# Keys and queries of the first parity by seven block products in place of eight

## The chip, the cores and the metric

The kernel runs on one core of a Trainium2 chip. The metric is device time in microseconds (us) for one execution of the whole program. Before the change three runs gave 600.47, 600.63 and 602.79 us, so the median is 600.63 us. The profile comes from one further execution, which took 599.87 us.

## The reference

The layer mixes a sliding, dilated attention (32 heads of 16 channels, a window of 8 keys, two positions apart) with a gated feed-forward layer. `x` is 2048 x 512 in float32.

```python
g = _sigmoid((x * gate_w).sum(-1, keepdims=True))
qkv = x @ wqkv                                  # 512 x 1536: keys, queries, values of 32 heads
logits = einsum("bhsd,bhswd->bhsw", q, k[idx]) * scale    # idx = pos - 2 * arange(8)
a = einsum("bhsw,bhswd->bhsd", softmax(logits), v[idx]) @ wo
b = (gelu(x @ w_gate) * (x @ w_up)) @ w_down              # F = 1792
return g * a + (1 - g) * b
```

## The kernel before

Each float32 operand of a matrix product is split into a high and a low part (`split`: a rounding copy `hi`, mostly on ACT, and a subtraction `lo = raw - hi`, mostly on DVE). A product then takes three matmuls: hi by hi, lo by hi, hi by lo.

Tokens are cut by parity (even and odd positions never attend to each other), and the kernel works through parity 0 and then parity 1, with 1024 tokens in each: two blocks of 512 tokens (`BT` = 4 tiles of 128). The 512 channels are four chunks `kc` of 128. The input `x` of a parity is a 2 x 2 block matrix: a11, a12 are block 0 with chunks 0-1 and 2-3, a21, a22 are block 1.

Several of the matrix products are done in Strassen's way, with seven block products in place of eight: the four sums s1 to s4 of x's blocks and t1 to t4 of the weight's blocks are made on DVE (`sum_x` or `sums_x`, `combine_b`, `make_v`, `combine`), split, and multiplied: a11 b11, a12 b21, s1 t1, s4 b22, s2 t2, s3 t3, a22 t4. This is how the values (`values`), the gate and up products (`gate_up`, L837) and the keys and queries of parity 1 (`keys`, `key_one`, `key_mm`) are computed. One block product of the keys and queries is 4 tiles x 2 chunks x 3 = 24 matmuls of 512 columns. One block product of the values is 24 matmuls of 258 columns.

The keys and queries of parity 0 go the plain way, in two halves of the heads (`hh`, weight blocks `cb` 0 and 2). The first half is the opening of the kernel: 8 tiles x 4 chunks x 3 = 96 matmuls (`qkv_mm`, L357), whose results `take_first` copies out, partly straight into the attention's tile `kq`. The second half is `project_one`, another 96 matmuls on L357, placed as `pieces` inside the first two of the 14 steps of the feed-forward loop (`ffn`, `gate_up`).

In order of the program: opening (L1109 to L1133), sums of x and the first three value operands, `values(0)` with its seven products (L408), the 14 feed-forward steps of parity 0 (products L778, down products L820), then `keys`, `values(1)` and the feed-forward steps of parity 1, the output product (L1050) and the end.

The attention itself runs on DVE (`scores`, `softmax`, `mix`: L569 to L622), in eight units: four of each parity. It is a generator from which the other code pulls: `pull(n)` adds n to a credit and emits attention instructions until their stated costs have used it up. The credits are constants in the code (`PACE` in the feed-forward steps, per parity). The first unit can start once the first half of the keys is there (`done.add((0, 0))`), it can only be mixed with the values once `values(0)` is through, and units 2 and 3 of a parity need the second half of the heads. Emitted attention instructions get a priority that lies 150 instructions behind (`BEHIND`).

A scheduler orders the instructions of each engine on a simulated timeline by priority; on the chip each engine runs its list in that order. SP issues nearly all loads and stores, POOL the ones that add into their destination. PSUM has eight banks: four of tag `p` and `acc0` to `acc3`. Tiles of one tag share a fixed number of buffers (`BUFS`), so a new tile waits until the old one's readers are done.

The steps to be followed: `room_v` says where the split value operands lie (tags `c`, `g1`, `g0`), `room_b` the same for key operands (`g1`, `d`), `load_v` and `load_b` load weights, `store_b` stores keys and queries, on POOL with an addition where a second product is added in DRAM.

Of the kernel before, what the change touches and what calls it, by code (L numbers as in the profile page):

```python
# [16 lines left out]
P = 128  # L17
# [15 lines left out]
PACE = (0.9, 1.22)  # L33
# [11 lines left out]
def tile_gated_mix(ctx: ExitStack, tc: tile.TileContext, xt, wqkv, wff, wo, out):  # L45
# [24 lines left out]
    idle = bank("p")  # L70
    for _ in range(WARM):
        nc.tensor.matmul(idle[:, :P], warm, warm, start=True, stop=True)
# [45 lines left out]
    def split_x(par, blk, kc, cols=((0, 512),), copy=None, pinned=False):  # L118
        if blk and kc < 2:
            X[par, blk, kc] = tl("rt", F32R), tl("rt", F32R)  # L120
# [6 lines left out]
    def sums_x():  # L127

        for n in ("s1", "s2", "s4", "s3"):
            for kc in range(2):  # L130
                XOP[n, kc] = pair("S")
        for kc in range(2):
            a11, a12, a21, a22 = (XR[kc][:, i * 512:(i + 1) * 512] for i in range(4))
            nc.vector.tensor_tensor(a22, a21, a22, op=OP.add)
            nc.vector.tensor_tensor(a21, a11, a21, op=OP.subtract)
            nc.vector.tensor_tensor(a11, a22, a11, op=OP.subtract)
            nc.vector.tensor_tensor(a12, a12, a11, op=OP.subtract)
            for n, x in ("s1", a22), ("s2", a11), ("s4", a12), ("s3", a21):
                split(nc.vector, *XOP[n, kc], x)
                yield  # L140

    def rooms():

        def of(*tags):
            for tag, n in tags:
                t = tl(tag, F32R)
                w = 512 if n == 4 else WA
                yield from (t[:, i * w:(i + 1) * w] for i in range(n))
        cols = of(("g1", 4))
        for _ in range(2):  # L150
            yield next(cols), next(cols)
        for _ in range(2):
            yield pair("S")
        for _ in range(KC):
            yield pair("d")

    def load_kq_weights(raw, kc):
        nc.sync.dma_start(raw[:, :512], wqkv[0, kc // 2, :, kc % 2 * 512:kc % 2 * 512 + 512])

# [3 lines left out]
    def load_cb(cb, kc, tag, room, late=False):  # L163
        hi, lo = WC[cb, kc] = next(room)
        raw = tl(tag)[:, :512]

        queue = nc.scalar if tag == "c" and not kc else nc.sync
        queue.dma_start(raw, wqkv[cb // 2, kc // 2, :, kc % 2 * 512:kc % 2 * 512 + 512])
        return lambda: split(nc.vector, hi, lo, raw, held if late else None)

    VW, VR, VO, SLOT = 2 * WQ, {}, {}, []

    def room_v(par):

        large, small = [("g1", 3), ("g0", 3)], [("c", 1)] * 4
        for tag, n in small + large if par else large[::-1] + small:
            t = tl(tag, F32R)
            SLOT.extend(t[:, i * WA:i * WA + VW] for i in range(n))  # L180
        for i, n in enumerate(("b11", "b21", "t1", "b22", "t2", "t3", "t4")):
            VO[n] = SLOT[i % 5 * 2:i % 5 * 2 + 2]
        SLOT.clear()

    def load_v():

        t = pool.tile([P, 2 * NP - 1, UC], F32, name="v").rearrange("p a c -> p (a c)")
        u = pool.tile([P, 2, BT * UC], F32, name="tb").rearrange("p a c -> p (a c)")
        places = [t[:, i * VW:(i + 1) * VW] for i in range(3)] + [u[:, :VW]]
        for n, raw in zip(("b11", "b21", "b12", "b22"), places):  # L190
            VR[n] = raw
            a, b = int(n[1]) - 1, int(n[2]) - 1
            nc.sync.dma_start(raw, wqkv[b, 2, :, a * VW:(a + 1) * VW])
# [78 lines left out]

    def sum_x(kc, n):
        a11, a12, a21, a22 = (XR[kc][:, i * 512:(i + 1) * 512] for i in range(4))
        o, a, b, op = {"s1": (a22, a21, a22, OP.add), "s3": (a21, a11, a21, OP.subtract),
                       "s2": (a11, a22, a11, OP.subtract), "s4": (a12, a12, a11, OP.subtract)}[n]
        paced(nc.vector.tensor_tensor(o, a, b, op=op))

    def split_s(n, kc, dma=False):
        i = {"s1": 3, "s2": 0, "s4": 1, "s3": 2}[n]  # L280
        raw = XR[kc][:, i * 512:(i + 1) * 512]
# [66 lines left out]
    names = iter(["p", "p", "acc0", "acc1", "p", "p", "acc2", "acc3", "acc0", "acc1", "acc2", "acc3", *["p"] * 4])  # L348
    stages = iter(["hh", "hl"] * 99)

    def qkv_mm(ps, par, jj, cb, kcs, c0=0, cn=512):
        t = slice((jj % BT) * P, (jj % BT + 1) * P)
        for kc in kcs:
            xh, xl = X[par, jj // BT, kc]
            wh, wl = WC[cb, kc]
            for n, (a, w) in enumerate(((xh, wh), (xl, wh), (xh, wl))):
                LAST[:] = [nc.tensor.matmul(ps[:, :cn], a[:, t], w[:, c0:c0 + cn], start=(kc == 0 and n == 0),  # L357
                                            stop=(kc == KC - 1 and n == 2))]
# [17 lines left out]
    def take(ps, par, jj, hh, tag=None):  # L376
        st = tl(tag or next(stages))[:, :512]
        nc.scalar.activation(st, ps, AF.Copy)
        two = st.rearrange("p (a c d) -> p a c d", a=2, c=2)
        queue = nc.scalar if par and not hh else nc.sync  # L380
        queue.dma_start(rows(KS[par, hh][:, W:], jj), two[:, 0])
        queue.dma_start(rows(QS[par, hh], jj), two[:, 1])

    def project(par, bg=iter(())):

        for jj in range(NP):
            ps = bank(next(names))
            qkv_mm(ps, par, jj, 0, range(KC))
            take(ps, par, jj, 0)
            next(bg, None)  # L390
            pull((2.7, 2.2)[par])
        done.add((par, 0))

    def values(par, bg, step):

        XOP.update(((n, kc), X[par, blk, kc + k]) for n, blk, k in (("a11", 0, 0), ("a12", 0, 2), ("a22", 1, 2))
                   for kc in range(2))
# [23 lines left out]
        for k, (a, b) in enumerate((("a11", "b11"), ("a12", "b21"), ("s1", "t1"), ("s4", "b22"), ("s2", "t2"),  # L421
                                    ("s3", "t3"), ("a22", "t4"))):
            for t in range(BT):
                if k == 0:
                    C[t] = bank(f"acc{t}")
                elif k == 2:
                    Z_[t] = bank("p")
                ps = Z_[t] if 0 < k < 4 else C[t]
                mm(ps, t, a, b, k in (0, 2))
                if k == 0:  # L430
                    Z_[t] = bank("p")
                    copy(Z_[t][:, :WQ], ps[:, :WQ])
                elif k == 2:
# [12 lines left out]
                else:  # L446
                    if k == 1:
# [8 lines left out]
        for _ in bg:  # L456
            pass
        done.add((par, 1))
# [6 lines left out]
    def keys(prep, bg):  # L465


        XOP.update(((n, kc), X[1, blk, kc + k]) for n, blk, k in (("a11", 0, 0), ("a12", 0, 2), ("a22", 1, 2))
                   for kc in range(2))
        C, Z_ = {}, {}  # L470
        for k, (a, b) in enumerate(KEYS[:5]):
# [7 lines left out]
            for t in range(BT):  # L479
# [5 lines left out]
                else:  # L485
# [3 lines left out]
                    store_b(nc.sync, st, t if k < 3 else BT + t, int(k in (2, 3)))  # L489
# [5 lines left out]
        done.add((1, 0))  # L495

# [12 lines left out]
    def store_b(queue, st, jj, hh, **kw):  # L509
        two = st.rearrange("p (a c d) -> p a c d", a=2, c=2)  # L510
        queue.dma_start(rows(KS[1, hh][:, W:], jj), two[:, 0], **kw)
# [727 lines left out]
```

## Time and profile before

| what | value |
|---|---|
| median of 3 runs | 600.63 us (600.47 to 602.79) |
| profiled execution, its own time | 599.87 us |
| its span, first to last instruction | 598.1 us |
| PE (matmul) busy | 591.2 us, 2767 matmuls |
| DVE busy | 535.2 us, 626 instructions |
| ACT busy | 417.4 us, 732 instructions |
| POOL busy | 90.6 us |
| moved by DMA | 135.68 MB |

A row of a group gives line, engine, operation, tiles and shapes, the count, then busy time and the mean of one in ns, then the engine's idle time ahead of them and what ended it. A row of the timeline or of the chain gives start and length in us. A row of the table by stretches gives the stretch, its length, and for each engine its busy time and count of instructions; then the granted clock, the mean share of the DMA engines and GB/s.

### The profile page before, as it was taken

The numbers are of one execution on the slowest core, as the hardware profiler recorded it, in microseconds if no ns is written. First come the engines' busy times: TensorE is split into PE (matmuls) and PEld (weight loads), VectorE is DVE, ScalarE is ACT, GpSimd is POOL, SyncE is SP. The second block draws the span as 40 slices with busy tenths as digits, with TensorE's granted clock in tenths as the row PEclk, the third lists the DMA queues.
The fourth block names the chain that finished last, engine by engine and source line by source line (L and its number), as shares of the span: only waits on it lengthen the run. The fifth ranks groups of instructions, "written<-read, shape, count | busy, mean of one in ns | idle before, by whom it ended". The sixth has DMA issues, their size and how long they took to land.

```text
span 598.1 us, 8231 instructions
## 1 busy us (share of the span) xinstructions
PE 591.2 (99%) x2767; PEld 494.3 (83%) x2767; DVE 535.2 (89%) x626; ACT 417.4 (70%) x732; POOL 90.6 (15%) x113
## 2 busy tenths in 40 slices
PE   9999999999999999999999999999999999999997
PEld 7898878888888887888889888888888888888885
DVE  6959899998999969998889998999799979999882
ACT  6664666678877787778777666566877678696722
POOL 0140000111111111103001472111111111121200
PEclk9999999999999999999999999999999999999999
DMA  8795996968687775898899999688968896878815
GB/s 280 255 262 176 295 316 201 274 175 268 187 225 210 228 216 166 228 310 283 268 269 325 243 299 272 203 215 238 257 145 194 239 257 151 219 184 220 109 39 175
DMA packets 90520, 135.68 MB, mean 227 GB/s; under 512 B 8431, under 2 KB 54895, under 8 KB 90478
## 3 DMA queue, kind: packets, MB, share of 16 engines
q1 hardware_dynamic: 70686, 102.98, 52.0%
q0 software_dynamic: 15152, 29.70, 28.0%
q10 hardware_dynamic: 4640, 2.49, 1.4%
q8 instruction: 21, 0.34, 0.2%
q14 instruction: 21, 0.17, 0.1%
HBM read 69.83 MB, written 42.56 MB: 188 GB/s over the span
## 4 chain that ended last, share of the span: by engine, by line
PE 87%; DMA 6%; ACT 4%; DVE 1%; issue 1%; SPq 0%; ACTq 0%; DVEq 0%
PE p L778 41%; PE p L820 13%; PE acc L820 12%; PE p L1050 5%; PE acc L506 5%; PE p L357 2%; PE p L408 2%; PE acc L357 2%; PE acc L1050 2%; PE acc L408 2%; DMA kq<-kq 1%; DMA ks<-hh 1%; PE p L506 1%; DMA vs<-hh 1%; DMA kq<-ks 1%
## 5 line engine op out<-in xcount | busy, mean ns | idle before, releaser
L778 PE MATMUL p<-S,g 128*128 128x512 f32 x672 | 168.7, 389 | 0.7 <-ACT s L783 0.7
L778 PEld LDWEIGHTS p<-S,g 128*128 128x128 f32 x672 | 125.8, 188 | 27.5 <-ACT s L783 1.5
L778 PE MATMUL p<-A,g 128*128 128x512 f32 x504 | 125.1, 389 | 0.4 <-ACT c L886 0.4
L778 PEld LDWEIGHTS p<-A,g 128*128 128x128 f32 x504 | 94.4, 188 | 20.3 <-ACT c L886 0.8
L569 DVE TENSOR_TENSOR prod<-kq 128x2048 f32<-128x2048 f32 x32 | 72.8, 2277 | 4.3 <-DMA kq<-kq 3.6
L609 DVE TENSOR_TENSOR prod<-v,lg 128x2048 f32<-128x2048 f32 x32 | 72.9, 2280 | 0.7
L572 DVE TENSOR_REDUCE lg<-prod 128x128 f32<-128x2048 f32 x32 | 73.0, 2281 | 0.1
L820 PE MATMUL p<-d,hh 128*128 128x512 f32 x224 | 68.6, 390 | 0.4 <-ACT p L814 0.4
L736 POOL DMA_DIRECT2D g<-raw x28 | 24.1, 862 | 255.0 <-ACT g L733 149.6
L820 PE MATMUL acc<-d,hh 128*128 128x512 f32 x224 | 59.9, 389 | 0.0
L789 ACT ACTIVATE c<-p 128x512 f32<-128x512 f32 x56 | 33.5, 597 | 34.1 <-PE p L778 34.0
L820 PEld LDWEIGHTS p<-d,hh 128*128 128x128 f32 x224 | 42.0, 188 | 9.4 <-ACT p L814 0.8
L820 PEld LDWEIGHTS acc<-d,hh 128*128 128x128 f32 x224 | 42.0, 188 | 8.7
L797 DVE TENSOR_TENSOR hl<-c,hh 128x512 fp32r<-128x512 f32 x56 | 38.4, 686 | 6.4 <-ACT hh L796 6.2
L820 PE MATMUL p<-d,hl 128*128 128x512 f32 x112 | 42.9, 389 | 0.0
L794 DVE TENSOR_TENSOR c<-c 128x512 f32<-128x512 f32 x56 | 38.3, 683 | 4.5 <-ACT c L886 4.5
L790 DVE TENSOR_TENSOR c<-c,s 128x512 f32<-128x512 f32 x56 | 38.1, 685 | 3.3 <-ACT c L789 3.3
L783 ACT ACTIVATE s<-p 128x512 f32<-128x512 f32 x56 | 33.0, 594 | 11.3 <-PE p L778 10.1
L769 POOL DMA_DIRECT2D d<-r x23 | 19.7, 856 | 130.3 <-ACT d L768 107.2
L613 DVE TENSOR_TENSOR prod<-prod 128x1024 f32<-128x1024 f32 x32 | 39.0, 1220 | 0.2
L796 ACT ACTIVATE hh<-c 128x512 fp32r<-128x512 f32 x56 | 35.1, 627 | 5.1 <-DVE c L794 4.8
L833 ACT ACTIVATE rt<-p 128x512 f32<-128x512 f32 x48 | 28.5, 596 | 11.9 <-PE p L820 11.6
(215 smaller groups left out, 1004.6 us busy)
## 6 DMA issues: line engine op xcount, KB each, us to landing
g<-raw POOLq DMA_DIRECT2D x28, 512.0 KB, 6.1
raw<-wff SPq DMA_DIRECT2D x42, 256.0 KB, 4.3
ws<-g SPq DMA_DIRECT2D x14, 768.0 KB, 5.5
g<-ws SPq DMA_DIRECT2D x14, 768.0 KB, 7.0
r<-wff SPq DMA_DIRECT2D x28, 256.0 KB, 4.1
d<-r POOLq DMA_DIRECT2D x23, 256.0 KB, 7.1
v<-vs SPq DMA_DIRECT2D x8, 512.0 KB, 7.7
os<-tb SPq DMA_DIRECT2D x64, 64.0 KB, 4.8
```

What stands on the lines that cost most here:

```text
L506: LAST[:] = [nc.tensor.matmul(ps, x[:, ts], w, start=(start and kc == i == 0), stop=(kc == 1 and i == 2), skip_group_check=True)]
L569: paced(nc.vector.tensor_tensor(prod, spans(k, jj), q[:, jj:jj + 2, None, :].to_broadcast([P, 2, W, UC]), op=OP.mult))
L572: nc.vector.tensor_reduce(two_of(lg, jj), prod.rearrange("p j w (h d) -> p (j w) h d", d=DH), axis=AX.X, op=OP.add)
L609: paced(nc.vector.tensor_tensor(prod.rearrange("p j w (h d) -> p (j w) h d", d=DH), spans(v, jj).rearrange("p j w (h d) -> p j w h d", d=D ...
L613: nc.vector.tensor_tensor(prod[:, :, :4], prod[:, :, :4], prod[:, :, 4:], op=OP.add)
L778: LAST[:] = [nc.tensor.matmul(ps, w_, a_, start=(start and kc == 0 and n == 0), stop=(kc == 1 and n == 2), skip_group_check=True)]
L790: nc.vector.tensor_tensor(c, c, s, op=OP.add)
L794: nc.vector.tensor_tensor(ge, ge, up, op=OP.mult)
L796: nc.scalar.activation(hh_, ge, AF.Copy)
L797: nc.vector.tensor_tensor(hl_, ge, hh_.bitcast(F32), op=OP.subtract)
L820: LAST[:] = [nc.tensor.matmul(pp, a[:, ts], w, start=(i == 0 and n == 0 and gr == 0), stop=(i == 1 and n == 2), skip_group_check=True)]
L1050: LAST[:] = [nc.tensor.matmul(pa, a, b, start=(first and n == 0), stop=(last and n == 2), skip_group_check=True)]
```

## The change

The keys and queries of parity 0 are computed by seven block products as well. Five of them (a11 b11, a12 b21, s2 t2, s3 t3, a22 t4) are done in the opening; the first two products of the values stand between the second and the third of them, and the other five products of the values follow. The last two (s1 t1, s4 b22) take the place of `project_one` in feed-forward steps 0 and 1 as `key_one(0, ...)`, whose results POOL adds into DRAM. With this, `sums_x`, `rooms`, `load_cb`, `qkv_mm`, `take`, `project` and `project_one` are gone. x's block a21 is no longer split. The first value product keeps its result in SBUF (`VB`) until the banks `acc0` to `acc3`, which the keys use until then, are free. The sum s1 goes to a tile of its own (tag `lg`), raw weights lie in the tile `prod`. The value operands take the small tiles (`c`) ahead of the large ones. The zero rows of K and V are written after the fifth product. The pace of the attention in parity 0 goes from 0.9 to 1.05, and the 31 warming matmuls are spread over four banks.

```diff
-PACE = (0.9, 1.22)
+PACE = (1.05, 1.22)
...
-    idle = bank("p")
-    for _ in range(WARM):
-        nc.tensor.matmul(idle[:, :P], warm, warm, start=True, stop=True)
+    idle = [bank("p") for _ in range(4)]
+    for i in range(WARM):
+        nc.tensor.matmul(idle[i // 4 % 4][:, i % 4 * P:(i % 4 + 1) * P], warm, warm, start=True, stop=True)
...
     def values(par, bg, step, ks=range(7)):
...
+            if k not in ks:
+                continue
             for t in range(BT):
                 if k == 0:
-                    C[t] = bank(f"acc{t}")
+                    C[t] = bank(f"acc{t}") if par else bank("p")
+                elif k == 1 and not par:
+                    Z_[t] = C[t]
                 elif k == 2:
                     Z_[t] = bank("p")
+                    if not par:
+                        C[t] = bank(f"acc{t}")
+                        copy(C[t][:, :WQ], VB.pop(t))
...
+                elif k == 0:
+                    VB[t] = tl("s" if t else "r")[:, :WQ]
+                    copy(VB[t], ps[:, :WQ])
...
     def ffn(par):
...
-            if par and f < 2:
-                pieces = [[lambda t=t: key_one(5 + f, t)] for t in range(BT)]
...
-            else:
-                pieces = [[lambda jj=jj: project_one(par, jj) for jj in jjs]
-                          for jjs in (((0, 1), (2, 3), (4, 5), (6,)), ((7,), (), (), ()))[f]]
+            if f < 2:
+                pieces = [[lambda t=t: key_one(par, 5 + f, t)] for t in range(BT)]
...
     for kc in range(KC):
+        name, i = ("b11", "b21")[kc // 2], kc % 2
+        if not i:
+            room_b(name)
...
+        raw = QR[name, i] = spare[i] if kc > 1 else tl("rt")
+        (nc.sync if kc else nc.scalar).dma_start(raw, wqkv[0, kc // 2, :, i * 512:i * 512 + 512])
+        for a, n in first:
+            o = kc // 2 * 512 + a
+            nc.sync.dma_start(XR[i][:, o:o + n], xt[0, :, kc, a:a + n])
+        for c in first:
+            split_x(0, 0, kc, (c,), None if kc else in_order)
+            if not c[0]:
+                split(nc.vector, *QO[name, i], raw)
+    set_x(0)
+    for kc in range(2):
+        nc.sync.dma_start(XR[kc][:, 1024:].rearrange("p (a c) -> p a c", a=2), xt[1, :, kc:kc + 3:2, :])
+        load_b("b22", kc, tl("rt"))
+        load_b("b12", kc, spare[2 + kc])
+        if not kc:
+            load_v("b11", "b21")
+    load_v("b12", "b22")
...
+    for kc in range(2):
+        for t in range(BT):
+            key_mm(C[t], t, *KEYS[0], (kc,), True)
+            if kc:
+                nc.scalar.activation(Z_[t], C[t], AF.Copy)
+    for kc in range(2):
+        for t in range(BT):
+            key_mm(Z_[t], t, *KEYS[1], (kc,), False)
+    for t in range(BT):
+        take_first(Z_[t], t, first_copy[t % 2])
+    room_v(*SMALL)
+    made = make_v()
+    for _ in range(2):
+        next(made)
+    room_b("t2")
...
+    for kc in range(2):
+        for n in "s1", "s3", "s2":
+            sum_x(kc, n)
+        split_s("s2", kc)
+        combine_b("t3", "b12", "b22", "b12", kc)
+        combine_b("t2", "b11", "t3", "b11", kc, OP.add)
+        split_b("t2", kc)
+    values(0, iter(()), lambda k: None, range(2))
+    room_b("t3")
+    for kc in range(2):
+        split_s("s3", kc)
+        split_b("t3", kc)
...
+    third(2)
+    room_b("t4")
+    for kc in range(2):
+        combine_b("t4", "b21", "b21", "t2", kc)
+        split_b("t4", kc)
+        split_x(0, 1, 2 + kc)
+    set_x(0)
+    for kc in range(2):
+        sum_x(kc, "s4")
+        split_s("s1", kc)
+        split_s("s4", kc)
+    third(3)
+    room_v(*LARGE)
+    store_v()
+    next(made)
+    for f in range(2):
+        fetch(f)
+    third(4)
+    done.add((0, 0))
+    PACING[0] = True
...
     def first():
-        for _ in range(6):
+        for _ in range(2):
             yield
         combine(0)
...
-        yield from last_weights()
+        fetch_d(0)
+        yield
+        for n in "t1", "b22":
+            room_b(n)
+            for kc in range(2):
+                if n == "t1":
+                    combine_b("t1", "b11", "b22", "t2", kc)
+                split_b(n, kc)
+                yield
...
-    values(0, first(), step)
+    values(0, first(), step, range(2, 7))
```

More of the change, by code (lines that the diff above doesn't have):

```diff
@@ L160, in held, with room_v @@
     def held(o, i):
         return paced(nc.scalar.activation(o, i, AF.Copy))
[L163 to L169, printed above, removed]
     VW, VR, VO, SLOT = 2 * WQ, {}, {}, []
-    def room_v(par):
-        large, small = [("g1", 3), ("g0", 3)], [("c", 1)] * 4
-        for tag, n in small + large if par else large[::-1] + small:
+    def room_v(*tags):
+        names = ("b11", "b21", "t1", "b22", "t2", "t3", "t4")
+        for tag, n in tags:
@@ L374, in rows, with values @@
         return t.rearrange("c (p j) d -> j p c d", j=NP)[jj]
[L376 to L397, printed above, removed]
+    VB = {}
+    def values(par, bg, step, ks=range(7)):
         C, Z_, PS, US, ST = {}, {}, {}, {}, {}
@@ new lines, in tile_gated_mix, with third @@
+    values(0, iter(()), lambda k: None, range(2))
[3 more added lines that the diff above has]
+        split_b("t3", kc)
+    def third(k, after=iter(())):
+        for kc in range(2) if k == 2 else (0,):
+            for t in range(BT):
+                key_mm(C[t], t, *KEYS[k], (kc,) if k == 2 else (0, 1), False)
+                if k == 2 and not kc:
+                    continue
+                if k == 4:
+                    take_first(C[t], BT + t, first_copy[t % 2])
+                else:
+                    st = tl(next(stages))[:, :512]
+                    nc.scalar.activation(st, C[t], AF.Copy)
+                    store_b(nc.sync, 0, st, t if k == 2 else BT + t, 1)
+                next(after, None)
```

158 lines of the change are left out of this document (46 added, 112 removed).

## The prediction

> **What bounds the kernel now.** I read the page first, then who PE waited for, then the table by stretches.
>
> ```profile
> span 598.1 us, 8231 instructions
> PE 591.2 (99%) x2767; PEld 494.3 (83%) x2767; DVE 535.2 (89%) x626; ACT 417.4 (70%) x732; POOL 90.6 (15%) x113
> ...
> PE 87%; DMA 6%; ACT 4%; DVE 1%; issue 1%; SPq 0%; ACTq 0%; DVEq 0%
> ```
>
> ```profile
> PE p L72 <- DVE warm L69: 1.0, 1, 1.0
> PE p L778 <- ACT s L783: 0.7, 1, 0.7
> PE p L778 <- ACT c L886: 0.4, 1, 0.4
> PE p L820 <- ACT p L814: 0.4, 1, 0.4
> PE p L408 <- ACT p L415: 0.3, 1, 0.3
> ```
>
> ```profile
> 27.00:50.00 23.00, 22.70 (x173) 21.72 (x172) 15.66 (x25) 13.80 (x39) 9.31 (x17) 1.00 0.75 221
> 50.00:72.00 22.00, 22.00 (x104) 18.23 (x103) 20.33 (x20) 14.75 (x29) 0.86 (x1) 1.00 0.85 249
> 72.00:87.00 15.00, 13.88 (x61) 10.88 (x59) 14.23 (x18) 7.77 (x13) 0.33 (x1) 1.00 1.05 352
> ...
> 90.00:282.00 192.00, 191.64 (x844) 158.06 (x843) 179.97 (x214) 147.41 (x239) 23.60 (x29) 1.00 0.79 228
> ```
>
> PE is the bound from end to end: 99% of the span, 87% of the chain, and all its waits for other engines come to 2.8 us. A matmul taken off PE is therefore worth its full pitch as long as nobody else becomes late. The one candidate is DVE. Its busy time is the fifth column of the stretches: over the feed-forward steps of parity 0 (90 to 282 us) it is 179.97 of 192 us, between 50 and 87 us 34.6 of 37 us.
>
> **The matmuls.** The mean of one (389 ns) is a latency; the pitch comes from the chain and the timeline, where matmuls stand back to back:
>
> ```profile
> L778 PE MATMUL p<-S,g 128*128 128x512 f32 x672 | 168.7, 389 | 0.7 <-ACT s L783 0.7
> ```
>
> ```profile
> 0.00:598.10 598.10, 45.69 (x192) 36.18 (x192) 1.00 0.82 227
> ```
>
> ```profile
> 282.17 5.44 PE acc L506 x24
> ...
> 316.87 3.22 PE p L408 x24
> ```
>
> The second fence is L357 alone: 192 matmuls, the plain product of both halves. Seven block products of 24 are 168 (120 in the opening, 48 in steps 0 and 1). So 24 matmuls of 512 columns go. The last fence starts with one such block product of parity 1: 24 in 5.44 us, 227 ns each. Removed: **5.44 us**. The values keep their 168 matmuls; one product takes 3.22 us, wherever it stands.
>
> The Trainium skill (TensorE: Matmul & The Clock Gate, Back-to-back issue gap) states a sustained 131 ns for a matmul of 512 columns in a stream, and 216 ns for an isolated one. By the first, 24 would be worth an estimated 3.1 us and the forecast would be 2.3 us higher. The trace does not agree: 5.44 us for 24.
>
> **The opening.** Before, 96 matmuls run from 4.27 us until the values' first at 26.92 us: 22.65 us for 96 x 0.227 = 21.8, so 0.9 us are lost to arriving data.
>
> ```profile
> 1.00 3.49 PE L72 MATMUL p<-warm 128*128 128x128 bf16 x31 [1.00 <-DVE warm L69]
> ...
> 4.27 1.78 PE L357 MATMUL p<-g,A 128*128 128x512 f32 x4
> ...
> 8.68 0.63 ACT L86 ACTIVATE A<-raw 128x512 fp32r<-128x512 f32 x1 [1.22 <-DMA raw<-xt]
> ...
> 26.92 2.31 PE L408 MATMUL acc<-g,A 128*128 128x258 f32 x18
> ```
>
> ```profile
> 4.00:5.00 1.00, 1.00 (x7) 0.73 (x6) 0.75 (x2) 0.21 (x1) 0.00 (x0) 1.00 0.79 266
> ...
> 7.00:8.00 1.00, 1.00 (x6) 0.82 (x5) 0.66 (x2) 0.46 (x1) 0.00 (x0) 1.00 0.87 215
> ...
> 9.00:10.00 1.00, 1.00 (x6) 0.82 (x5) 0.65 (x1) 0.83 (x2) 0.00 (x0) 1.00 1.04 395
> ```
>
> The start needs the same first chunk, and the warming matmuls keep their number: 0, within 0.2 us either way for the other banks. After, a chunk feeds 12 matmuls (2.72 us) instead of 24, so chunk 1 is wanted earlier: at 4.27 + 0.9 + 2.72 = 7.9 us. It came at 8.68 us, behind block 1's chunk 0 (0.26 MB, 1.2 us at 215 GB/s), which now comes later; so about 7.5 us, and 8.1 us after its 0.63 us copy. I keep the 0.9 us of loss: change 0, bounds -0.9 and +1.5.
>
> Then the first two value products. Ahead of their weights SP asks for 2.1 MB of chunks and key weights, 0.52 MB of x's block 1, 0.52 MB of key weights and 0.53 MB of their own: 3.67 MB. With 1.05 MB there at 7.5 us, 0.5 MB more by 9 us and then 395 GB/s, they land at about 14.4 us; copy and subtraction (0.63, 0.69) make 15.7 us, and PE comes at 4.27 + 0.9 + 10.88 = 16.05 us. Margin 0.35 us: I take 0.3 us of stall, bounds 0 and 2.
>
> **Sums and splits.**
>
> ```profile
> L789 ACT ACTIVATE c<-p 128x512 f32<-128x512 f32 x56 | 33.5, 597 | 34.1 <-PE p L778 34.0
> ...
> L797 DVE TENSOR_TENSOR hl<-c,hh 128x512 fp32r<-128x512 f32 x56 | 38.4, 686 | 6.4 <-ACT hh L796 6.2
> L794 DVE TENSOR_TENSOR c<-c 128x512 f32<-128x512 f32 x56 | 38.3, 683 | 4.5 <-ACT c L886 4.5
> L790 DVE TENSOR_TENSOR c<-c,s 128x512 f32<-128x512 f32 x56 | 38.1, 685 | 3.3 <-ACT c L789 3.3
> ...
> L705 DVE TENSOR_TENSOR raw<-raw 128x256 f32<-128x256 f32 (+1 forms) x42 | 21.2, 506 | 2.9 <-DMA raw<-wff 2.7
> ...
> L729 DVE TENSOR_TENSOR g<-raw,g 128x768 fp32r<-128x768 f32 x14 | 13.3, 953 | 2.3 <-ACT g L725 2.3
> ```
>
> ```profile
> 45.66 2.29 DVE L569 TENSOR_TENSOR prod<-kq 128x2048 f32<-128x2048 f32 x1 [3.62 <-DMA kq<-kq]
> ...
> 294.08 1.89 DVE L87 TENSOR_TENSOR S<-raw,S 128x512 fp32r<-128x512 f32 x3
> ```
>
> Key weights need 14 splits for 8 (+6), 8 sums of weight blocks (+8), x two splits fewer (-2): 12 operations of 512 columns on DVE. The last row has three in 1.89 us, a pitch of 0.60 us: **7.2 us more for DVE**. Between 16 and 25 us the second chunk of s2 and t2 needs seven of them (4.2 us) after its data at about 17 us, so 21 to 22 us, and PE wants it at 16.05 + 6.4 + 2.7 = 25.2 us. Later operands have the margin of 2 to 3 us: cost 0. ACT gets 4 splits, 4 + 4 copies between banks and SBUF, and 8 evacuations of 0.6 us (L789), 12 us more of its 180 us of idle time: 0. SP's 16 stores of the second half stay 16, only earlier; POOL gets 16 adding stores, on a queue that carried the same for parity 1 (the `ks<-rt` row of POOL below, x8 for keys and again for queries); there the five products run without a gap (the last row):
>
> ```profile
> raw<-wff SPq DMA_DIRECT2D x42, 256.0 KB, 4.3
> ...
> ks<-rt POOLq DMA_DIRECT2D x8, 128.0 KB, 9.6
> ```
>
> ```profile
> 282.00:309.20 27.20, 27.20 (x121) 22.52 (x120) 24.75 (x36) 20.52 (x39) 2.17 (x4) 1.00 0.84 261
> ```
>
> SP's fetch of the first feed-forward weights needs the `raw` buffers of x, free only after s4's split (about 36 us); 4.3 us later it is there, some 15 us before step 0 begins at about 55 us: 0. The zero rows move past the fifth product on POOL's queue, and the operand sum of step 0 stands behind them; 9.3 us of POOL from 40 us still end before that: 0.
>
> **Cover.** Before, 96 matmuls that need nobody (the second half, 21.8 us) lie around steps 0 and 1, where DVE is full; still PE lost 1.1 us between 72 and 87 us. After, there are 48, and the `c` tiles are held by values until their last product, so of step 0 only three products can be drawn ahead. I take 1.0 us more, bounds -1.1 (those waits vanish) and +4 (one 1.1 us wait in each of the next steps too).
>
> **Attention.** Scoring began at 45.66 us, when the two small transfers inside `kq` had landed:
>
> ```profile
> 38.66 6.92 DMA kq<-kq
> ```
>
> After, the five key products and two value products end at 16.35 + 6.4 + 16.3 = 39 us; copies and that transfer bring scoring to about 47 us (up to 52 if SP's queue is held once more). That is 1 to 6 us later, while DVE still has sums of the values to make. From there DVE must find 7.2 + 5.44 us in what it left idle between 50 and 282 us: 2.4 us to 87 us, 12.0 us from 90 us, 14.4 in all for 12.6. The code's credits say the same: a step emits 4.1 x 1.05 + 4 x 1.26 = 9.35 us of attention for 8.0 before; the eight pulls of 2.7 in `project_one` (21.6) become eight of 1.1 (8.8). In sum over parity 0 about as much as before, but at a fuller DVE. I take 0 here, since it fits; it is a rival below.
>
> **Sum.** -5.44 + 0.3 + 1.0 = -4.1 us. The profiled execution, 599.87 us (span 598.1 and 1.8 around it), becomes 595.7 us; it lies 0.76 us below the median of the runs, so **596.5 us**.
>
> **Rivals.**
> *Data or operands late in the opening.* Were everything to land at 266 GB/s (the 4 to 5 us row) instead of 395, the value weights would come at 17.4 us, split 18.7 us, 2.7 us after PE, with chunk 1 of s2 following late. 596.5 + 2.4 = 599 us. For it: a margin of 0.35 us. Against it: 395 GB/s held as soon as requests were queued.
> The Trainium skill (TensorE: Matmul & The Clock Gate, HAM oscillation) has a further step: a PE pause above 3.4 us halves the clock until it has been busy that long again. Here the granted clock is 1.00 in every stretch quoted and the longest wait 1.0 us; it would be an estimated 1.7 us on top, only if the pause grew so long.
>
> *The removed matmuls were filling.* If steps 0 and 1 wait for DVE anyway, taking 24 fillers away only uncovers the wait: nothing gained, 600.6 us. For it: DVE at 34.6 of 37 us there. Against: most of that is attention, which gives way.
>
> *DVE becomes the bound in parity 0.* By durations a step needs 6 x 0.685 + 3 x 0.506 + 0.953 = 6.6 us for itself, with 9.35 us of attention 15.95 us, against 66 matmuls = 14.96 us: 1.0 us too much in ten steps, 10 us, so 595.2 + 10 = 605 us, slower. By the pitch (0.60) it needs 5.8 + 9.35 = 15.1 us, less where large operations overlap too, and fits. It decides from the point where a step's DVE time exceeds 15 us by more than 0.8 us over ten steps. Before, the same count by durations gives 14.6 us and DVE had idle left, which speaks for the pitch.
>
> **How the numbers follow.** Forecast 0.62 (593 to 597.5 us), late opening 0.12, uncovered wait 0.11, DVE the bound 0.15. A measurement of this kernel can tell about 0.5% (3 us) from no change, so faster means below 597.6 us: 0.62; the two middle cases are the same: 0.23; slower 0.15. The range leaves out most of the DVE rival and goes down to the full saving without the 2 us of old waits: 593 to 602 us.
>
> **What would show it.** PE: 2743 matmuls, busy near 586 us. Right: the value products begin near 16 us, the fifth key product ends near 39 us, no wait above 1 us there. Cover: waits of L778 on ACT or DVE between 55 and 100 us of about 2 us. The attention at the end of parity 0 as far as before, 5 us earlier. Wrong if PE waits for L790 or L797 repeatedly after 90 us, if its last third has gaps that end with attention, or if the opening has a gap of 2 us on V weights.

## The result and the profile after

The changed kernel takes 622.25 us (median of 4 runs, 621.61 to 624.31) against 600.55 us: ratio 1.036, interval 1.032 to 1.039. It is slower by 21.7 us. The forecast was 596.5 us with a range up to 602, so both the sign and the range were wrong.

The page of the kernel after: span, busy time by engine, the granted clock in 40 slices of 15.5 us, and the chain by engine.

```profile
span 620.4 us, 8250 instructions
PE 597.5 (96%) x2743; PEld 494.7 (80%) x2743; DVE 540.7 (87%) x637; ACT 432.5 (70%) x755; POOL 110.5 (18%) x129
...
PEclk9989988999999999999979999999999999999999
...
PE 65%; DVE 13%; issue 8%; ACT 6%; DMA 6%; SPq 1%; ACTq 0%; POOL 0%; DVEq 0%; POOLq 0%
```

PE has 24 matmuls fewer, as planned, but 6.3 us more of busy time: the same work runs at a lower clock in places (the 3rd, 6th, 7th and 21st slice). The chain now spends 13% on DVE, which was 1%. Who PE waited for, after:

```profile
PE acc L458 <- ACT S L126: 6.0, 2, 3.4
PE p L725 <- ACT c L736: 4.6, 3, 3.5
PE acc L458 <- ACT z L352: 2.4, 1, 2.4
PE acc L458 <- DVE S L87: 1.7, 2, 0.9
PE acc L345 <- DVE g L87: 1.4, 1, 1.4
```

L458 is the matmul of the keys' block products, L345 that of the values, L725 the feed-forward one. To place the loss I counted matmuls by stretch (second column of numbers: PE's busy time and count), before and after:

```profile
0.00:120.00 120.00, 117.58 (x605) 99.94 (x606) 104.42 (x142) 75.31 (x145) 15.74 (x29) 1.00 0.84 257
120.00:270.00 150.00, 149.64 (x660) 123.28 (x659) 139.96 (x165) 118.09 (x191) 16.27 (x19) 1.00 0.77 222
...
300.00:598.10 298.10, 293.98 (x1374) 246.26 (x1372) 265.28 (x284) 200.01 (x353) 52.51 (x55) 1.00 0.82 213
```

```profile
0.00:120.00 120.00, 106.36 (x520) 87.61 (x521) 87.92 (x128) 81.30 (x155) 33.86 (x43) 0.94 0.87 240
120.00:270.00 150.00, 148.86 (x655) 122.50 (x654) 139.34 (x167) 116.18 (x186) 17.13 (x20) 1.00 0.78 219
...
270.00:330.00 60.00, 55.75 (x231) 44.48 (x231) 55.72 (x69) 39.77 (x72) 6.99 (x11) 0.94 0.80 241
...
322.00:620.40 298.40, 294.55 (x1376) 246.73 (x1374) 265.77 (x284) 200.53 (x354) 52.50 (x55) 1.00 0.82 213
```

By 120 us the kernel before has done 605 matmuls, of which 24 no longer exist; the one after has done 520. It is 61 behind, at 0.227 us 13.8 us. Five more (1.1 us) go until 270 us. The spans differ by 22.3 us, so 7.4 us are left for what comes later; the last 1376 matmuls take 298.4 us after and the last 1374 took 298.1 us before, which puts all of it ahead of 322 us, at the turn of the parities. So two places lose: **the opening and the first steps, 13.8 us (19 us with the 5.4 us saved), and the turn, 7.4 us.** The experiments are given in the same three parts.

The first place, PE's timeline of the kernel after (start, length, line, count, in brackets the wait before it):

```profile
16.85 3.74 PE L345 MATMUL p<-c,A 128*128 128x258 f32 x30
...
28.16 1.49 PE L458 MATMUL acc<-g,S 128*128 128x512 f32 x4 [2.65 <-ACT S L126]
30.52 3.78 PE L458 MATMUL acc<-g,S 128*128 128x512 f32 x8 [0.87 <-DVE S L87]
34.10 6.39 PE L458 MATMUL acc<-d,S 128*128 128x512 f32 x24
...
79.54 7.35 PE L458 MATMUL acc<-d,S 128*128 128x512 f32 x24 [2.42 <-ACT z L352]
...
103.07 2.17 PE L725 MATMUL p<-A,g 128*128 128x512 f32 x6 [3.49 <-ACT c L736]
105.04 2.63 PE L725 MATMUL p<-S,g 128*128 128x512 f32 x6
```

The values begin where forecast (16.85 for 16.05 us), with no wait for their weights. Then PE waits 2.65 us for the second chunk of the sum s2, and soon after it eight matmuls take 3.78 us, which take 2.12 us where the clock stays full (the version with fillers, below); the next 24 take 6.39 instead of 5.62. The granted clock from 28 to 34 us is 0.57. Each longer wait is followed by such a slow group.

### The profile page after: what moved, and what is told of

Same layout as the page of the kernel before. It is cut to its first block, busy times and chain, and to the rows that moved or that the text cites. A ratio compares the mean times of both kernels' runs of the same rounds, so it can differ in the third digit from the quotient of the medians.

```text
span 620.4 us, 8250 instructions
## 1 busy us (share of the span) xinstructions
PE 597.5 (96%) x2743; PEld 494.7 (80%) x2743; DVE 540.7 (87%) x637; ACT 432.5 (70%) x755; POOL 110.5 (18%) x129
## 4 chain that ended last, share of the span: by engine, by line
PE 65%; DVE 13%; issue 8%; ACT 6%; DMA 6%; SPq 1%; ACTq 0%; POOL 0%; DVEq 0%; POOLq 0%
PE p L725 31%; PE acc L767 9%; PE p L767 8%; PE acc L458 7%; PE p L992 5%; PE p L345 2%; PE acc L992 2%; DVE prod L551 1%; PE acc L345 1%; DVE raw L242 1%; DMA raw<-xt 1%; DVE prod L511 1%; DMA vs<-hl 1%; DVE lg L514 1%; DMA r<-wff 1%
## 5 line engine op out<-in xcount | busy, mean ns | idle before, releaser
L725 PE MATMUL p<-S,g 128*128 128x512 f32 x672 | 170.6, 391 | 0.5 <-ACT s L730 0.5
L725 PEld LDWEIGHTS p<-S,g 128*128 128x128 f32 x672 | 126.7, 189 | 27.2 <-ACT s L730 0.9
L725 PE MATMUL p<-A,g 128*128 128x512 f32 x504 | 127.2, 391 | 4.6 <-ACT c L736 4.6
L725 PEld LDWEIGHTS p<-A,g 128*128 128x128 f32 x504 | 94.2, 188 | 25.5 <-ACT c L736 5.9
L511 DVE TENSOR_TENSOR prod<-kq 128x2048 f32<-128x2048 f32 x32 | 72.9, 2279 | 2.7 <-DMA kq<-kq 2.6
L744 DVE TENSOR_TENSOR hl<-c,hh 128x512 fp32r<-128x512 f32 x56 | 38.4, 687 | 6.8 <-ACT hh L743 6.8
L737 DVE TENSOR_TENSOR c<-c,s 128x512 f32<-128x512 f32 x56 | 38.1, 685 | 4.7 <-ACT c L736 4.0
L716 POOL DMA_DIRECT2D d<-r x23 | 19.7, 858 | 123.4 <-ACT d L715 102.8
L458 PE MATMUL acc<-d,S 128*128 128x512 f32 x144 | 37.6, 410 | 2.4 <-ACT z L352 2.4
```

What stands on the lines that cost most here:

```text
L458: LAST[:] = [nc.tensor.matmul(ps, x[:, ts], w, start=(start and kc == i == 0), stop=(kc == 1 and i == 2), skip_group_check=True)]
L511: paced(nc.vector.tensor_tensor(prod, spans(k, jj), q[:, jj:jj + 2, None, :].to_broadcast([P, 2, W, UC]), op=OP.mult))
L725: LAST[:] = [nc.tensor.matmul(ps, w_, a_, start=(start and kc == 0 and n == 0), stop=(kc == 1 and n == 2), skip_group_check=True)]
L737: nc.vector.tensor_tensor(c, c, s, op=OP.add)
L744: nc.vector.tensor_tensor(hl_, ge, hh_.bitcast(F32), op=OP.subtract)
```

## Experiments

The runs come in groups, each with the kernel before run beside it; its median lay between 599.4 and 601.0 us. A difference of two times from different groups is therefore uncertain by some 1.5 us; the ratios allow for it.

**Order or clock in the opening.** Why is that chunk late? DVE's timeline of the kernel after:

```profile
18.92 0.68 DVE L242 TENSOR_TENSOR lg<-raw 128x512 f32<-128x512 f32 x1
...
20.73 0.69 DVE L87 TENSOR_TENSOR A<-raw,A 128x512 fp32r<-128x512 f32 x1
21.33 0.69 DVE L232 TENSOR_TENSOR prod<-rt,prod 128x512 f32<-128x512 f32 x1
...
25.55 0.69 DVE L165 TENSOR_TENSOR v<-tb,v 128x516 f32<-128x516 f32 x1
26.15 0.69 DVE L87 TENSOR_TENSOR g<-prod,g 128x512 fp32r<-128x512 f32 x1
26.76 0.69 DVE L242 TENSOR_TENSOR raw<-lg,raw 128x512 f32<-128x512 f32 x1
```

The first and last rows are the second chunk's sums s1 and s2. Between them stand twelve operations that DVE runs back to back, and none of its operations from 13 to 35 us waits for a transfer: it is not late data. s2 needs one of the twelve (s3, which is made from the same buffers), two more make the second chunk of t2, which the third product needs as well, and the other nine belong to the first chunk, to the values and to later products. One edit holds the opening's sums and splits to program order; another fills the pause with work that needs nobody, to keep the clock.

```
# e3: each sum and split of the opening stands, in DVE's list, behind the one before it in the program
-    paced(nc.vector.tensor_tensor(o, a, b, op=op))
+    chained(paced(nc.vector.tensor_tensor(o, a, b, op=op)))
```

> The changed kernel with the sums and splits of the keys' operands in the opening held to program order on DVE (an order, no wait), so that the second chunk of s2 and t2 comes 8 operations earlier. Theory 'order': the third product waited for DVE work that stood behind work wanted later; the waits for S in the third product (3.5 us) and the half clock behind them (some 3 us) vanish, the fifth product ends at 40 to 42 us instead of 46.9, and the time falls by 5 to 7 us to 615 to 617 us. Rival 'data': block 1 of x lands too late for any order, and the fifth product still ends after 45 us.

614.9 us, ratio 1.025 (1.022 to 1.028): 7.3 us better than the kernel after. Yet the third product does not go on earlier. From the timelines of DVE, ACT and PE of this run:

```profile
22.98 0.69 DVE L254 TENSOR_TENSOR raw<-lg,raw 128x512 f32<-128x512 f32 x1
...
24.35 0.38 ACT L364 ACTIVATE hh<-p 128x256 f32<-128x256 f32 x1 [2.08 <-PE p L357]
24.63 0.17 ACT L364 ACTIVATE z<-p 128x1 f32<-128x1 f32 x1
24.68 0.63 ACT L127 ACTIVATE S<-raw 128x512 fp32r<-128x512 f32 x1
...
27.59 0.64 ACT L127 ACTIVATE g<-rt 128x512 fp32r<-128x512 f32 x1
...
28.29 4.48 PE L470 MATMUL acc<-g,S 128*128 128x512 f32 x12 [2.35 <-ACT g L127]
```

The sum s2 is made 3.8 us earlier, but its copy then stands in ACT's list behind an evacuation of the values that waits 2.08 us for PE, and the weights' copy comes last. What the order gained is the second wait and some clock: the fourth product ends at 38.5 us for 40.5, the fifth at 44.9 us, not at the 40 to 42 us expected.

```
# e5: in third(), between the two chunks of the third product
+    for _ in range(14):
+        tc.keep_in_program_order(nc.tensor.matmul(DUMMY[0], hi[:, :P], w, start=True, stop=True))
```

> The changed kernel with 14 matmuls of 512 columns more (3.2 us of PE work whose result nobody reads) between the two chunks of the third product, where PE pauses 2.65 us. Theory 'clock': the pause costs the clock, and matmuls that fill it keep it; products three and four then run at 227 ns (5.4 us for 24, not 6.4), and the fifth product ends 1.5 to 3 us earlier although PE does more; time 619 to 621 us. Rival: the granted clock falls for another reason, the added matmuls only add, the fifth product ends up to 1 us later, time 622 to 623 us.

614.7 us, ratio 1.025 (1.022 to 1.028): 7.5 us better, with 14 matmuls more. In its timeline the fillers (L1113) stand in the pause:

```profile
25.17 3.34 PE L1113 MATMUL p<-d,A 128*128 128x512 f32 x14
28.34 1.07 PE L458 MATMUL acc<-g,S 128*128 128x512 f32 x4
30.33 2.12 PE L458 MATMUL acc<-g,S 128*128 128x512 f32 x8 [0.92 <-DVE S L87]
32.29 5.62 PE L458 MATMUL acc<-d,S 128*128 128x512 f32 x24
```

The third product goes on at the same time as in the kernel after, 28.3 us, yet the fourth ends 2.6 us earlier (37.9 for 40.5): that is the clock nearly alone, since DVE's part of the last operand came only 0.2 us earlier. The fifth ends 2.1 us earlier (44.8 for 46.9), within the 1.5 to 3 us expected. The larger part of the gain comes later: the waits of 2.42 us for z and 3.49 us for c, with the slow groups behind them, are absent here and with the order held. Why they go when the values begin two microseconds earlier is not shown.

> The changed kernel with both edits tried singly: DVE's sums and splits of the opening held to program order, and fourteen filling matmuls of 512 columns (result unread) between the two chunks of the third key product. Each alone gave 7.4 us. If both act through the same pause (it ends on DVE's late chunk, and it makes the granted clock fall), together they give no more than the longer of them and a little: 612 to 615 us, and the third product follows the fillers without a wait above 1 us. If order and clock are separate losses the gains add up: 606 to 609 us. In both cases the wait of about 4.9 us for ACT S L126 at the turn of the parities (295 to 312 us) stays.

615.3 us, ratio 1.025 (1.022 to 1.027). The gains do not add up: with both, the third product runs on without a wait, but waits of 1.95, 2.28 and 2.79 us stand further on (for the values' parts and the keys' copy).

**The value stores.** ACT stood 8.9 us behind its own stores of values before z.

```
-            queue = nc.sync if par else nc.scalar
+            queue = nc.sync
```

> The changed kernel with the value stores of parity 0 on SP's queue instead of ACT's. Theory: ACT's instruction queue stands 8.9 us behind a store of values that waits for its transfer (79.32 us, ACT z L352) and PE loses 2.4 us there and, later, 3.5 us on c L736 at 103 us. Then the first of these waits goes and the clock of 79 to 87 us returns: 616 to 619 us. Rival: the transfers of values are late in any queue, and SP's own stores of the keys come behind them: 621 to 624 us, the wait named differently.

622.3 us, ratio 1.036 (1.032 to 1.041): no gain. The wait for z is gone, and waits of 2.69 us (for the keys' copy) and 4.67 us (for weights, behind a transfer) stand at 97 and 112 us instead. ACT's blocked queue was not the cause by itself. This run shows one thing more: its pause in the third product was 2.20 us, the granted clock behind it stayed at 1.00, and the fourth product ended at 37.7 us, as early as with the fillers. None of that was left at 120 us (table below), so the clock of the opening alone does not explain the 7.5 us that the fillers gave.

**The pace.** The change also raises the pace at which attention is emitted. That is undone here, and done alone in the kernel before.

```
-PACE = (1.05, 1.22)
+PACE = (0.9, 1.22)     # e1; the reverse in the kernel before for e2
```

> The changed kernel with the attention's pace of parity 0 back at 0.9. Theory 'pace': the 8.1 us lost at the turn of the parities (290 to 322 us) come from scores that the faster pace puts on DVE just when the second parity's key operands are due, so the waits for s2 vanish and the time falls by 6 to 8 us, to 614 to 616 us. Rival 'late start': the attention is behind because it starts 9 us later and has less cover, whatever the pace; then the waits stay and the time stays within 2 us of 622, or the end waits for the attention and it gets longer. Everything up to 54 us should be as in the changed kernel.

641.5 us, ratio 1.071 (1.067 to 1.075): 19 us worse, not 6 to 8 us better; the rival had the end right. The turn is little better (243 matmuls between 270 and 330 us for 231), and the end waits for attention; the two largest waits of PE:

```profile
PE p L992 <- ACT hh L86: 8.4, 1, 8.4
PE acc L992 <- ACT hh L86: 5.0, 1, 5.0
```

> The kernel before with only the pace of parity 0 raised to 1.05. Theory 'pace': it overfills DVE there too, PE waits at the turn of the parities, 603 to 609 us. Rival: DVE of the kernel before has the room, and the time stays at 600 to 602 us.

620.8 us, ratio 1.037 (1.031 to 1.044). Up to 270 us it has done as many matmuls as the kernel before, to within one; by 400 us it is 79 behind, 17.9 of the 20.4 us that it loses. The lengths of DVE's attention instructions (L569 to L622) add up to 51.2 us by 120 us and 88.1 us from there to 270 us; in the kernel before it was 51.1 and 88.3 us. So in parity 0 a higher pace brings no attention forward: DVE is nearly full there (139.96 of 150 us from 120 to 270 us in the kernel before), and what is emitted above that piles up and is run at the turn, among the sums and splits of parity 1's keys. What is not emitted is missing at the end.

**The turn.** In the kernel after, scoring stands in DVE's list ahead of the sums of parity 1's keys (L242); in the kernel before the first scoring there comes at 298.97 us, behind the first six of those sums (L277, 284.47 to 291.10 us).

```profile
289.75 2.29 DVE L511 TENSOR_TENSOR prod<-kq 128x2048 f32<-128x2048 f32 x1
...
296.62 2.29 DVE L511 TENSOR_TENSOR prod<-kq 128x2048 f32<-128x2048 f32 x1
...
305.23 0.69 DVE L242 TENSOR_TENSOR raw<-raw 128x512 f32<-128x512 f32 x1
```

In the version with fillers no attention is emitted from the last two steps of parity 0:

```
-    pull(n * PACE[par] * (1.0 if par or f + 1 < FC else 0.8))
+    pull(n * PACE[par] * (1.0 if par or f + 2 < FC else 0.0))
```

> The version with the fourteen filling matmuls (614.7 us), in which the last two feed-forward steps of parity 0 emit no attention (4.3 + 3.4 us of credit less ahead of the turn of the parities; the same attention comes later). Theory: at the turn DVE makes scoring pairs of 4.5 us each between the sums and splits of parity 1's keys, because attention is late there; without them the waits of 1.55 and 4.86 us at 295 to 306 us shrink to under 1.5 us in all and the granted clock of 300 to 330 us goes from 0.94 to 1.00: 6 to 8 us less there. The 7.7 us of attention come out at the end: at no cost if the end has room (607 to 609 us), in full if it has none (waits for ACT hh L86 at the end, 612 to 616 us). Rival: the turn waits for the operands' transfers or for ACT whatever DVE does: the 4.9 us wait stays, 614 to 615 us.

626.3 us, ratio 1.043 (1.041 to 1.045). The 4.86 us wait at the turn is gone and its clock is back, but the end pays: `hh` of attention is waited for with 9.3 and 1.7 us, and 11.6 us are lost against the version with fillers. What I gave as "at no cost if the end has room" did not come about; the end has none.

> Order of the opening held, fillers in the pause, no attention in the last two steps of parity 0, and parity 1's pace at 1.25 for 1.22 (3.7 us of credit more over fourteen steps). By the theories of the opening and of the turn: 604 to 609 us, with no wait above 3 us between 290 and 320 us. If lower than 599 us the change would pay after all; I expect not, since the opening keeps 5 us or more of its loss.

628.1 us, ratio 1.045 (1.041 to 1.049), with the same end (9.1 and 2.2 us). The raised pace of parity 1 did not make it good.

**Is it DVE's time?** First DVE work was added to the kernel before, which has neither the new opening nor the late attention:

```
+    for _ in range(1 if not par and 0 < f < 9 else 0):     # e12; 2 in e13
+        paced(nc.vector.tensor_tensor(lo, raw, hi.bitcast(F32), op=OP.subtract))
```

> The kernel before, with one subtraction of 768 columns (0.87 us of DVE, its result unchanged) made twice in each of steps 1 to 8 of parity 0: 7.0 us more for DVE, about what the change adds to it, and nothing else. By the prediction's sum it fits into what DVE left idle (14.4 us between 50 and 282 us) and costs 0: 600 to 601.5 us. By the theory that DVE has no room in parity 0 (attention, which comes last on it, falls behind and is made up at the turn of the parities or at the end): 603 to 609 us, with waits on ACT or DVE between 280 and 310 us or on ACT hh at the end.

602.25 us, ratio 1.003 (1.001 to 1.004): 1.7 us for 7.

> The same with three subtractions instead of one: 14 us more for DVE in parity 0, about the change's 7.2 us and the 5.4 us that PE's span should have lost. By the prediction's sum just within the idle time: 600 to 603 us. By the theory that DVE has no room: 607 to 616 us, at least 4 us more than with 7 us.

606.8 us, ratio 1.010 (1.007 to 1.012): 6.2 us for 14. The first 7 us nearly fit, as the prediction reckoned; of the second 7 most comes out. So the load of the change (7.2 us) by itself costs little, at least in steps 1 to 8, where this load was put; most of the change's own stands earlier. What makes the rest is taken up after the next runs.

Then attention was taken away from the version with fillers, first early (e14), then where DVE is full (e16, e17):

```
+            if (par, u) in ((0, 2),) and jj > 2:     # e16; unit (0, 0) in e14, (0, 1) and (0, 2) in e17
+                yield 4.6
+                continue
```

> The version with the fourteen filling matmuls (614.7 us), with two of the four scoring pairs of the first attention unit left out (the scores there are set to zero by POOL): 9.0 us less for DVE in parity 0, at the same emission of attention. By the theory that attention is late for want of DVE's time: the waits of 1.55 and 4.86 us at the turn of the parities shrink to under 3 us in all and nothing comes out at the end: 607 to 610 us. Rival, that the turn waits for something else than DVE: 614 to 615 us.

612.45 us, ratio 1.019 (1.016 to 1.021): 2.3 us better (3.9 by the ratios). Between 72 and 90 us DVE was busy 7.71 of 18 us, for 12.66: it idled where the work had been, and the turn kept its loss.

> The version with the fourteen filling matmuls (614.7 us), with two of the four scoring pairs of the third attention unit of parity 0 left out (their scores are set to zero by POOL): 9 us less for DVE between 200 and 270 us, where it is full. If attention is late for want of DVE's time, the waits of 1.55 and 4.86 us at the turn fall below 3 us in all: 607 to 611 us. If the turn waits for something else: 614 to 615 us.

608.5 us, ratio 1.012 (1.008 to 1.016).

> The same with two pairs of the second unit left out as well: 18 us less for DVE between 120 and 270 us. By the theory the turn has no wait above 1 us and its granted clock is 1.00; also the waits of 1.2 and 0.4 us near 250 us go: 604 to 607 us. What is left above the kernel before is then the opening. By the rival: 613 to 615 us.

604.05 us, ratio 1.005 (1.003 to 1.007). At the turn of e17, L458's five products follow at 5.44 us without a wait:

```profile
284.77 5.60 PE L458 MATMUL acc<-g,A 128*128 128x512 f32 x24
290.21 5.60 PE L458 MATMUL p<-d,A 128*128 128x512 f32 x24
295.65 5.60 PE L458 MATMUL acc<-g,S 128*128 128x512 f32 x24
301.09 5.60 PE L458 MATMUL acc<-d,S 128*128 128x512 f32 x24
```

The same place in the version with fillers, and in the kernel after:

```profile
294.96 5.76 PE L458 MATMUL p<-d,A 128*128 128x512 f32 x24 [1.55 <-ACT p L432]
305.58 7.11 PE L458 MATMUL acc<-g,S 128*128 128x512 f32 x24 [4.86 <-ACT S L126]
```

```profile
311.45 1.47 PE L458 MATMUL acc<-g,S 128*128 128x512 f32 x4 [3.37 <-ACT S L126]
313.80 7.26 PE L458 MATMUL acc<-g,S 128*128 128x512 f32 x20 [0.88 <-DVE S L87]
```

Nine microseconds of DVE give 6.2, eighteen give 10.6 (7.7 and 11.9 by the ratios), and from 270 us on nothing is lost any more (table below). That settles the turn: the attention that is still to be done by 270 us is what it loses its time to.

Where does it fall behind? From the first scoring to 120 us, before and after:

```profile
45.66:120.00 74.34, 73.22 (x337) 60.40 (x336) 71.74 (x80) 45.60 (x80) 5.11 (x6) 1.00 0.85 251
```

```profile
54.20:120.00 65.80, 57.80 (x268) 47.09 (x267) 53.62 (x65) 45.35 (x79) 25.56 (x24) 0.95 0.95 237
```

Added up as above, attention (L511 to L564 in the kernel after) had 30.2 us by 120 us, for 51.1 before, and 87.9 us from there to 270 us, for 88.3. So the arrears of 21 us arise by 120 us and are not made up. In the two stretches DVE is busy 18.1 us less than before: 8.5 us because scoring starts later, 9.6 us because DVE stands idle more after that (12.2 us for 2.6). No run starts scoring earlier, so what an earlier start alone would give is not shown.

Two real edits for the same relief, on the version with fillers: the weight sums on POOL, and the low part of the weights by a negated copy on ACT and an adding transfer.

```
-    sub = lambda o, a, b: paced(nc.vector.tensor_tensor(o, a, b, op=OP.subtract))             # e15
+    sub = lambda o, a, b: paced((nc.gpsimd if f > 1 else nc.vector).tensor_tensor(o, a, b, op=OP.subtract))
+    paced(nc.scalar.activation(lo, raw, AF.Copy, scale=-1.0))                                  # e18
+    nc.gpsimd.dma_start(lo.bitcast(F32), raw, accum_op=OP.add)
```

> The version with the fourteen filling matmuls, with the weight sums of the feed-forward steps from the third on (three per step, 1.4 us of DVE) made by POOL: 20 us less for DVE in parity 0. If POOL makes them in its idle time (it is busy 18%) without holding DVE up, attention catches up, the turn has no wait and the time is 605 to 609 us; if both are slowed by one another or the sums come late for their subtraction, 613 to 625 us, with waits on the operands of the first product of a step. Less than 599 us would make it a version that beats both kernels; I give that one chance in ten.

628.5 us, ratio 1.046 (1.043 to 1.048). The turn has no wait left, but the steps wait: POOL needs 2.06 us for a sum of 512 columns and 1.46 us for 256 (DVE 0.68 and 0.42), and DVE's own operations of 512 columns in a step (L737 to L744) last 0.75 to 1.11 us in the mean beside it, for 0.69 with fillers. Between 120 and 270 us ACT waits 11.2 us for POOL's sums and 19.7 us for DVE's `c` (3.1 with fillers), PE waits for ACT, and it does 591 matmuls for 653.

> The version with the fourteen filling matmuls, with the low part of each step's first weight group in parity 0 (from step 2 on) made as the second group's is: ACT writes the negated copy and a transfer adds the weights to it. DVE loses 12 subtractions of 0.87 us, 10.4 us; ACT gets 12 copies of 0.85 us and the queues twelve adding transfers of 0.39 MB. If DVE's time is what parity 0 lacks and the transfers have room: 607 to 611 us. If ACT or the transfers are then late: 615 to 622 us, with waits on weights of the first product of a step.

611.6 us, ratio 1.018 (1.014 to 1.022): 3.1 us better (4.3 by the ratios). The turn gains 6 us; the first steps lose 4 to late weights. Neither beats the kernel before.

In the three parts, as time behind the kernel before (matmuls missing at 120 and at 270 us times 0.227 us, without the 24 and the fillers; the rest is the difference of spans less these). The spans are of the one profiled execution of each run, which for e16 took 1.1 us more and for e17 1.6 us less than the median:

```
                     to 120 us   120 to 270   from 270    sum
after                   13.8        1.1          7.4      22.3
stores on SP (e4)       14.1        0.2          8.4      22.7
order held (e3)          6.1        1.6          8.5      16.2
fillers (e5)             4.5        1.6          7.9      14.0
  - 9 us early (e14)     5.9       -0.9          8.4      13.4
  - 9 us (e16)           5.9        1.4          2.4       9.7
  - 18 us (e17)          3.6       -0.7         -0.3       2.6
  no late pulls (e9)     5.0        1.4         19.7      26.1
  low part by ACT (e18)  8.6        0.9          2.0      11.5
pace 0.9 (e1)           15.2        1.1         24.8      41.1
before, pace (e2)        0          0.2         20.4      20.6
```

## Why the prediction was wrong

*The matmuls: right.* 24 are gone, and where PE runs freely a product of 24 still starts 5.44 us after the one before.

*Start of the opening and of the values: right.* 16.85 us for 16.05; the bounds (-0.9 and +1.5, 0 and 2) hold it.

*"Sums and splits ... margin of 2 to 3 us: cost 0": failed, the first of two.* The sum put the second chunk of s2 and t2 ready at 21 to 22 us: seven operations from 17 us on, as if DVE and ACT had nothing else. The third product went on with it at 28.2 us (28.3 in the other order, e3), because the first chunk's operations and those of the values share the two lists. PE's pause is 3.5 us with 2.6 us of slow clock behind it; of the 19 us lost by 120 us the edits at this place give back 7.7 and 9.3 (table).

*The clock: mis-sized.* The prediction let it count only from a pause above 3.4 us, at 1.7 us. The pause of 2.65 us brought 2.6 us of slow matmuls by the end of the fourth product (40.5 us for 37.9 with fillers).

*Cover 1.0 us: too small.* From 57 to 103 us five waits come to 8.0 us, above the bound of 4. The two largest are absent in e3 and e5, which leave the cover as it is, so want of cover alone does not make them. With fillers the opening is 4.5 us behind and the 5.4 us saved are gone too: of these 9.9 us, 3.2 us are the pause in which the fillers stand and 6.1 us are seven waits of 0.7 to 1.0 us each. Those seven I did not take apart.

*ACT +12 us at 0:* the waits are named after ACT, but with the stores off its queue the time did not move (e4). Whether ACT's copies alone cost anything stays open; putting them on DVE wasn't tried.

*"Attention ... I take 0 here, since it fits": failed, the second.* Scoring began at 54.2 us, above the 52 given as the limit and 8.5 us later than before. The sum set needs of 12.6 us against idle time of 14.4 us, as if all of it could be had. Even in the kernel before 7 us more cost 1.7 us and 14 us cost 6.2 us (e12, e13), and idle time that lies before scoring can start, or in holes of DVE's list, is of no use to attention (e14). By 120 us attention was 21 us behind, and it came out as 7.4 us at the turn.

*The rivals.* "DVE becomes the bound in parity 0" (605 us, 0.15) had the right engine and the wrong place: between 120 and 270 us the steps lose 1.1 us in all; attention, last in DVE's list, gives way and collides with the keys of parity 1. "Late opening" (599 us) had the place, with data named instead of the lists of DVE and ACT, and 2.4 us for the 13.8 us measured. I had set them as alternatives; they came together.

## What to carry to other kernels

An operand's time is its place in the lists of all engines that make it, not the sum of the operations that it needs: before giving a margin, count everything that must pass there in the same stretch. Where a filler stream takes all the slack of an engine, its backlog is a debt: slowing it down or speeding it up only moved the payment between the next bottleneck and the end here, and of what was tried in parity 0 only less work where DVE is full lowered it. A pause on PE can cost nearly twice its length (2.65 us and 2.6 us of slow matmuls here), and matmuls with no reader in it can be worth more than they cost (the fifth product ended 2.1 us earlier with them).

## What was not expected of the hardware

The granted clock fell after some pauses of PE of 2.4 to 3.5 us. In the kernel after, behind waits of 2.65, 2.42 and 3.49 us, eight matmuls took 3.78 us (2.12 in e5), 24 took 7.35 (5.60 in e17) and six took 2.63 (1.52 elsewhere in the kernel after). The granted clock was 0.57 from 28 to 34 us, 0.79 from 79 to 87 us and 0.66 from 103 to 108 us. Other pauses of that length cost nothing, as at the turn in e9, where it was 1.00 from 296 to 303 us:

```profile
296.86 5.73 PE L458 MATMUL p<-d,A 128*128 128x512 f32 x24 [2.91 <-ACT p L432]
```

The Trainium skill (TensorE: Matmul & The Clock Gate, HAM oscillation) asks for no idle gaps above about 3.4 us; Part 1 of the page calls the window free-running. As a safe limit the first does not hold here: pauses of 2.42 and 2.65 us were followed by slow matmuls. That pauses of the same length did and did not cost the clock would fit the second, if it matters where in the window a pause falls, but no run here shows the window.
